# Seven block products instead of eight in the last ten slices of the first feed-forward

## The chip, the core and the metric

The kernel runs on one core of one Trainium2 chip. The metric is device time of one execution, in microseconds, as the median of three runs. TensorE (PE) multiplies; VectorE (DVE), ScalarE (ACT) and GpSimd (POOL) work on vectors; SyncE (SP) issues the DMAs.

## The reference

Windowed attention over 2 x 8 heads of 768 positions (windows of 96 keys and 24 block summaries), then two feed-forwards over the 1536 token rows of width 512 that it gives. The core of the reference, everything in float32:

```
h = x @ w_in          # 1536 x 512 by 512 x 2048
g = h * np.cos(h)     # first feed-forward
g = h * np.clip(h + 3.0, 0.0, 6.0) / 6.0   # second feed-forward
x = g @ w_out         # 1536 x 2048 by 2048 x 512
```

The weights come in as float64 in memory (512 KB for each slice of 128 x 512) and are brought to float32 on the chip by integer operations.

## The kernel before

**Precision and tiling.** Each float32 operand of a product is split into a high part in the engine's reduced float32 format and a rest ("hi" and "lo"), and a product is three passes: hi by hi, lo by hi, hi by lo. The 1536 token rows are three blocks of 512 (0, 1, 2); the inner width of 2048 is 16 slices of 128. A step is one slice by one block: its first product (12 matmuls of 512 columns into one PSUM bank, `mm1`), its middle (the nonlinearity, then the split of g, `middle`) and its second product (12 matmuls of 512 columns into four accumulators, `mm2`). Two steps make what the text calls a pair-block: two slices by one block.

**Groups and runs.** `GROUPS` cuts the 16 slices into groups; within a group all blocks are passed, forwards or backwards, and the four accumulators stay in PSUM for a run of steps of the same block. When a run closes, four "sums" add the accumulators to `total` in SBUF. The first group's steps on blocks 0 and 1 are made in halves of 256 columns while the attention still runs.

**Seven products.** The whole second feed-forward makes the first products of two slices together: the pair of weight slices and the block of x are each cut two by two, four sums of weights and four sums of x ("pair sums", "tees") are formed beforehand, and seven products of 256 columns (`mm1_set`, 7 x 6 matmuls) with one copy ("take") and five DVE additions ("add") give both slices' h in `hs`, in SBUF. The step `SETS` is the first one done so. Before it, h is read from PSUM directly.

**Order.** Nothing is written in its final order. Every operation is put into a graph with the engines that may run it and their costs; a planner gives each a due time from its successors plus a lead for its kind (`LEAD`, two numbers: before and after the attention's buffers are given up), and then forms every engine's queue by due time. Each engine runs its own queue strictly in order. Where the plan shows a gap on PE, filler matmuls of a zero tile are put in (`fill`); the threshold is a number in `run`. Of two engines that may run an operation (DVE or POOL, DVE or ACT) the planner chooses.

**Buffers.** Two pair buffers `phi`/`plo` hold the split weights of two pairs (or of six single slices), two buffers `raw`, `cv_y` and `cv_t` serve all weight conversions in turn, the g buffers number four plus one lent from `tx` (the sums of x), and in the sets h and c have four and three buffers.

The lines of the profile that the text names: L836 first products one slice at a time, L787 block products, L954 second products, L800 adds, L901 to L914 the middle of a step (turns, rest, cosine, gate, g hi, g lo), L487 to L515 the conversion of a weight slice, L455 its lo part, L472 pair sums, L741 to L754 tees, L924 and L929 fillers, L992 sums, L616 to L700 attention.

Of the kernel before, what the change touches and what calls it, by code (L numbers as in the profile page):

```python
# [36 lines left out]
class Graph:  # L37
# [18 lines left out]

    LEAD = {
        "add": (0.0, -9.5), "block product": (0.0, -0.9), "carry": (43.6, 0.3), "cosine": (2.4, 0.0),
        "flip": (1.4, 0.0), "g hi": (0.9, 0.0), "g lo": (0.4, -6.4), "gate": (2.3, 7.0), "gate six": (0.0, -60.9),
        "hi": (-2.2, -167.1), "identity": (4.0, 0.0), "inverse": (2.1, 0.0), "join": (5.5, 0.0),  # L60
        "key maxima": (165.5, 0.0), "largest": (-4.4, 0.0), "lo": (12.0, -0.3), "load v": (8.8, 0.0),
        "load window": (1.5, 0.0), "mask": (33.2, 0.0), "masks": (-4.3, 0.0), "means back": (5.9, 0.0),
        "means out": (-0.1, 0.0), "means over": (39.5, 0.0), "pair sums": (0.0, -72.4), "power": (5.3, 0.0),
        "put k": (-17.0, 0.0), "put v": (9.5, 0.0), "rebias": (-9.5, -7.7), "rest": (-30.7, 5.6),
        "scaled": (3.8, 0.0), "scores": (-2.4, 0.0), "second": (9.7, 15.7), "shift": (2.9, 0.0), "sign": (23.1, 4.6),
        "sums": (0.0, 1.4), "take": (0.0, 3.0), "tees": (0.0, -3.1), "tees hi": (0.0, 19.3), "tees lo": (0.0, 6.5),
        "turns": (0.0, 16.9), "wake": (4.4, 0.0), "weighted": (1.4, 0.0), "weights": (0.0, 0.6),
        "window": (253.9, 0.0), "x hi": (0.1, 0.0), "x lo": (-10.8, 0.0), "y lo": (0.0, -2.4),
# [87 lines left out]
    def replay(self, on, order):  # L156
# [8 lines left out]
        for _ in range(n):  # L165
            best = None
            for e, queue in queues.items():
# [7 lines left out]
                t = max(t, free.get(e, 0.0))  # L175
                if e == "POOL" or (e == "DVE" and self.twice[i]):
                    t = max(t, port)
                if best is None or t < best[0]:
                    best = (t, e, i)
            t, e, i = best  # L180
# [10 lines left out]
    def run(self):  # L191
# [17 lines left out]
        for i, j in zip(pe, pe[1:]):  # L209
            after[i] = max(0, int((begins[j] - ends[i] - 0.9) / mm(512)))  # L210
# [33 lines left out]
def attention_two_ffn(  # L244
# [32 lines left out]
    GROUPS = ((3, 3, 3, 3, 4), (4, 4, 4, 4))  # L277
    plan = []
    for m in range(2):
        f0 = 0  # L280
        for g, n in enumerate(GROUPS[m]):
            for b in range(NBLK) if (g + m * (len(GROUPS[0]) + 1)) % 2 == 0 else reversed(range(NBLK)):
# [9 lines left out]
    SETS = next(s for s in range(NSTEP) if plan[s][0])  # L292
# [164 lines left out]

    def convert_pair(p):

        if 2 * p >= len(slices):  # L460
            return
        i = p % NPAIR

        (y1, t1, y1k, t1k), (y0, t0, y0k, t0k) = nearest(2 * p, "in"), nearest(2 * p + 1, "in")
# [9 lines left out]
        for c0, c1, x, k in ((0, 2, y0.bitcast(F32), y0k), (2, 3, a22, y1k),  # L474
                             (3, 5, t0.bitcast(F32), t0k), (5, 7, t1.bitcast(F32), t1k)):
            hi, lo = (lambda t=t, c0=c0, c1=c1: t[i][:, c0:c1, :].rearrange("p a c -> p (a c)") for t in (phi, plo))
            also = [(n, "in", PER * i + f) for n in ("whi", "wlo") for f in range(PER)] if p < NF // 2 + NPAIR else []
# [123 lines left out]
    def front(u):  # L601
# [67 lines left out]
        G.op("inverse", {"DVE": 0.33}, inverse, r=[("sm", si)], w=[("rs", si)], twice=True)  # L669
# [97 lines left out]

    def mm1_set(s, due):

        m, blk, f, _, _ = plan[s]  # L770
        p = slices.index((m, f)) // 2
        i = p % NPAIR
# [299 lines left out]
    gone = set()  # L1072
# [20 lines left out]
    for what, s in events:  # L1093
# [16 lines left out]
        elif s == uses[m, f]:  # L1110
            now = s
            if n < NF - PER * NPAIR:
                convert(n + PER * NPAIR, "in")
            elif n < NF:

                gone.add(n % (PER * NPAIR))
                for i in range(NPAIR):
# [3 lines left out]
            elif n % 2:  # L1121
                convert_pair(n // 2 + NPAIR)
# [57 lines left out]
```

## Time and profile before

| | |
|---|---|
| median of 3 runs | 598.93 us (598.66 to 598.95) |
| the profiled execution | 598.99 us, span 597.2 us |
| mean granted clock of PE | 0.994 |
| PE busy | 582.4 us (98%) |
| DVE busy | 460.6 us (77%) |
| ACT busy | 344.1 us (58%) |
| POOL busy | 190.6 us (32%) |

Times within a trace are from the first instruction on. The first step in full width begins at about 94 us, the last attention unit's PE work ends at about 109 us, block products begin at 322 us, and the last matmul starts at 592.9 us. A busy time counts an instruction from its start to its end as recorded; since the next one on the same engine often starts before that end, the distance from start to start is the better price.

### The profile page before, as it was taken

The numbers are of one execution on the slowest core, as the hardware profiler recorded it, in microseconds if no ns is written. First come the engines' busy times: TensorE is split into PE (matmuls) and PEld (weight loads), VectorE is DVE, ScalarE is ACT, GpSimd is POOL, SyncE is SP. The second block draws the span as 40 slices with busy tenths as digits, with TensorE's granted clock in tenths as the row PEclk, the third lists the DMA queues.
The fourth block names the chain that finished last, engine by engine and source line by source line (L and its number), as shares of the span: only waits on it lengthen the run. The fifth ranks groups of instructions, "written<-read, shape, count | busy, mean of one in ns | idle before, by whom it ended". The sixth has DMA issues, their size and how long they took to land.

```text
span 597.2 us, 10065 instructions
## 1 busy us (share of the span) xinstructions
PE 582.4 (98%) x3818; PEld 498.8 (84%) x3818; DVE 460.6 (77%) x828; ACT 344.1 (58%) x721; POOL 190.6 (32%) x184
## 2 busy tenths in 40 slices
PE   9987999999999999999999999999999999999997
PEld 5666689888888888888888898989989889898985
DVE  5885898999877967755658998999998768963552
ACT  4887889787645635533447765667465445442320
POOL 4365544244403202101213554332534033411200
PEclk9988999999999999999999999999999999999999
DMA  8975323423412311301200220332322121100103
GB/s 308 308 250 167 99 89 91 154 69 137 134 37 70 107 36 35 106 1 36 71 1 1 72 65 7 106 106 72 141 68 75 70 72 36 37 0 1 54 37 124
DMA packets 17009, 51.51 MB, mean 86 GB/s; under 512 B 1984, under 2 KB 1984, under 8 KB 16960
## 3 DMA queue, kind: packets, MB, share of 16 engines
q1 hardware_dynamic: 16960, 50.86, 25.6%
q8 instruction: 30, 0.49, 0.3%
q14 instruction: 19, 0.16, 0.1%
HBM read 47.71 MB, written 3.15 MB: 85 GB/s over the span
## 4 chain that ended last, share of the span: by engine, by line
PE 89%; DMA 4%; DVE 3%; ACT 2%; issue 1%; SPq 0%; ACTq 0%; DVEq 0%
PE bank_a L954 22%; PE bank_d L836 12%; PE bank_d L787 10%; PE bank_b L954 10%; PE bank_c L954 10%; PE bank_c L787 5%; PE bank_e L787 5%; PE bank_c L836 5%; PE bank_e L836 5%; PE bank_e L700 2%; PE bank_b L685 2%; PE bank_c L629 1%; DMA raw<-in_w_out_dram 1%; DMA total<-in_vw_dram 1%; DMA raw<-in_w_in_dram 1%; DMA vnat<-in_vw_dram 1%
## 5 line engine op out<-in xcount | busy, mean ns | idle before, releaser
L515 POOL TENSOR_TENSOR cv_y<-cv_t,cv_y 128x512 int32<-128x512 int32 x30 | 43.3, 1449 | 90.8 <-DVE cv_t L513 61.9
L914 POOL TENSOR_TENSOR glo<-ch_c,ghi 128x512 fp32r<-128x512 f32 x21 | 28.3, 1348 | 123.8 <-PE bank_c L954 69.3
L438 ACT CAST ghi<-ch_c 128x512 fp32r<-128x512 f32 x57 | 35.4, 620 | 47.9 <-PE bank_c L954 47.1
L513 DVE SCALAR_TENSOR_TENSOR cv_t<-raw,cv_t 128x512 int32<-128x512 int32 x64 | 48.6, 769 | 0.4
L908 ACT ACTIVATE ch_c<-hs,three 128x512 f32<-128x512 f32 x48 | 34.5, 722 | 18.9 <-DVE hs L800 18.5
L506 ACT ACTIVATE cv_t<-raw 128x512 f32<-128x512 f32 x52 | 35.0, 676 | 16.4 <-DMA raw<-in_w_out_dram 7.4
L496 ACT ACTIVATE cv_y<-raw 128x512 int32<-128x512 uint32 x53 | 35.4, 673 | 14.5 <-POOL wlj_out L455 5.2
L910 DVE SCALAR_TENSOR_TENSOR ch_c<-ch_c,hs 128x512 f32<-128x512 f32 x48 | 40.3, 846 | 2.7 <-ACT ch_c L908 2.4
L800 DVE TENSOR_TENSOR hs<-bank_d,hs 128x256 f32<-128x256 f32 x60 | 25.1, 419 | 20.7 <-PE bank_d L787 19.9
L914 DVE TENSOR_TENSOR glo<-ch_c,ghi 128x512 fp32r<-128x512 f32 x44 | 35.4, 806 | 1.4 <-PE bank_c L954 0.9
L836 PE MATMUL bank_d<-xlo,phi 128*128 128x512 f32 (+1 forms) x136 | 35.6, 358 | 0.0
L836 PE MATMUL bank_d<-xhi,phi 128*128 128x512 f32 (+1 forms) x136 | 32.3, 360 | 2.4 <-DVE ch_e L905 2.2
L511 DVE TENSOR_SCALAR cv_t<-cv_t 128x512 int32<-128x512 int32 x64 | 29.5, 468 | 2.7 <-ACT cv_t L506 2.7
L836 PE MATMUL bank_d<-xhi,plo 128*128 128x512 f32 (+1 forms) x136 | 31.5, 356 | 0.0
L836 PEld LDWEIGHTS bank_d<-xhi,phi 128*128 128x128 f32 x136 | 23.4, 193 | 6.4 <-DVE ch_e L905 2.5
L660 ACT ACTIVATE es<-bank_c,nmx 128x120 f32<-128x120 f32 x80 | 27.6, 370 | 1.8 <-DVE nmx L653 1.6
L515 DVE CUSTOM_DVE_ANT_0 cv_y<-cv_t,cv_y 128x1024 uint16<-128x1024 uint16 x34 | 26.2, 772 | 2.2 <-ACT cv_y L496 2.1
L836 PEld LDWEIGHTS bank_d<-xlo,phi 128*128 128x128 f32 x136 | 23.8, 193 | 3.7 <-issue 0.2
L992 DVE SCALAR_TENSOR_TENSOR total<-bank_a,total 128x512 f32<-128x512 f32 x22 | 14.8, 686 | 15.5 <-PE bank_a L954 15.3
L836 PEld LDWEIGHTS bank_d<-xhi,plo 128*128 128x128 f32 x136 | 23.4, 193 | 3.5
L455 POOL TENSOR_TENSOR plo<-cv_y,phi 128x512 fp32r<-128x512 f32 (+1 forms) x16 | 19.8, 1238 | 15.1 <-ACT phi L438 14.4
L903 ACT ACTIVATE ch_c<-ch_c,half_pi 128x512 f32<-128x512 f32 x25 | 18.1, 722 | 9.1 <-DVE ch_c L901 9.1
(348 smaller groups left out, 1838.2 us busy)
## 6 DMA issues: line engine op xcount, KB each, us to landing
raw<-in_w_in_dram SPq DMA_DIRECT2D x32, 512.0 KB, 3.3
raw<-in_w_out_dram SPq DMA_DIRECT2D x32, 512.0 KB, 3.3
vcat<-in_vw_dram SPq DMA_DIRECT2D x12, 384.0 KB, 4.6
ktile<-in_kt_dram SPq DMA_DIRECT2D x8, 384.0 KB, 5.9
qt<-in_q_dram SPq DMA_DIRECT2D x12, 256.0 KB, 4.3
out_dram<-total SPq DMA_DIRECT2D x8, 256.0 KB, 2.0
total<-in_vw_dram SPq DMA_DIRECT2D x6, 256.0 KB, 6.2
out_dram<-totak SPq DMA_DIRECT2D x4, 256.0 KB, 2.0
```

Of the source, the lines that this page charges most:

```text
L438: nc.scalar.copy(o, i) if e == "ACT" else VEC[e].tensor_copy(o, i)
L496: nc.scalar.activation(y, low.bitcast(U32), AF.Copy, scale=2.0 ** -29)
L506: nc.scalar.activation(o, a, AF.Copy, scale=2.0 ** -112)
L511: G.op("shift", {"DVE": dve(DM, 2)}, lambda e: nc.vector.tensor_scalar(t, t, 3, None, ALU.logical_shift_left), w=[tk], twice=True)
L513: G.op("sign", {"DVE": dve(DM)}, lambda e: nc.vector.scalar_tensor_tensor(t, high, -0x80000000, t, ALU.bitwise_and, ALU.bitwise_or), r=[rk ...
L515: G.op("join", {"POOL": pool(DM), "DVE": dve(DM)}, lambda e: VEC[e].tensor_tensor(y, t, y, ALU.add), r=[tk], w=[yk], twice=True)
L787: nc.tensor.matmul(o, wt[i][:, A[a], kk * P:(kk + 1) * P], xt[:, kk, :], start=first and n + kk == 0, stop=n + kk == 3, skip_group_check=True)
L836: nc.tensor.matmul(h, w["in"][i][:, kk * P:(kk + 1) * P], x[blk][:, kk, c0:c1], start=p + kk == 0, stop=p == 2 and kk == NK - 1)
L908: G.op("relu", {"ACT": act(N) + 0.1}, lambda e: nc.scalar.activation(c(), h(), AF.Relu, bias=three), r=hk, w=ck)
L910: G.op("gate six", {"DVE": dve(N)}, lambda e: nc.vector.scalar_tensor_tensor(c(), c(), 6.0, h(), ALU.min, ALU.mult), r=hk, w=ck, twice=boo ...
L914: G.op("g lo", {"DVE": dve(N), "POOL": pool(N)}, lambda e: VEC[e].tensor_tensor(gbuf("lo", s)[:, 0:N], c(), gh().bitcast(F32), ALU.subtrac ...
L954: nc.tensor.matmul(acc(s, i)[0], l, r, start=first, stop=end and p == 2 and (N == TOK or i % 2 == 1), skip_group_check=N < TOK)
```

## The change

Ten of the 16 slices of the first feed-forward are made by pairs as in the second: `WHOLE` = 6 slices stay single, and `SETS` moves from the first step of the second feed-forward to the first step of slice 6. The groups become 3, 3, 4, 2, 4; the blocks' direction is a table (`BACKWARD`), so that the second and third group start at block 0 again. The sums of x for the first feed-forward are formed from the hi and lo parts of x (`tees_of_parts`), in the buffers that the second feed-forward uses later. The lent g buffer is used up to four steps ahead of `SETS`. `inverse` is two operations instead of one. The planner lets an operation take the port that DVE and POOL share 0.055 us early, breaks ties by when an operation was ready, has other leads for its kinds, and puts fillers into gaps from 0.3 us beyond a filler's own length instead of 0.9.

```
+    HANDED = 0.055
     LEAD = {
-        "add": (0.0, -9.5), "block product": (0.0, -0.9), "carry": (43.6, 0.3), "cosine": (2.4, 0.0),
+        "add": (0.0, -116.7), "block product": (0.0, 0.3), "carry": (6.7, 17.2), "cosine": (-4.2, -220.4),
...
                 if e == "POOL" or (e == "DVE" and self.twice[i]):
-                    t = max(t, port)
+                    t = max(t, port - self.HANDED)
...
-            after[i] = max(0, int((begins[j] - ends[i] - 0.9) / mm(512)))
+            after[i] = max(0, int((begins[j] - ends[i] - 0.3) / mm(512)))
...
-    GROUPS = ((3, 3, 3, 3, 4), (4, 4, 4, 4))
+    GROUPS = ((3, 3, 4, 2, 4), (4, 4, 4, 4))
+    BACKWARD = ((0, 0, 0, 1, 1), (1, 0, 1, 0))
+    WHOLE = GROUPS[0][0] + GROUPS[0][1]
...
-    SETS = next(s for s in range(NSTEP) if plan[s][0])
+    SETS = next(s for s in range(NSTEP) if plan[s][0] or plan[s][2] >= WHOLE)
...
-        def inverse(e):
-            nc.vector.tensor_scalar(sme, sm, 1.0e-9, None, ALU.add)
-            nc.vector.reciprocal(rs, sme)
+        G.op("sum", {"DVE": 0.13}, lambda e: nc.vector.tensor_scalar(sme, sm, 1.0e-9, None, ALU.add),
+             r=[("sm", si)], w=[("sme", si)], twice=True)
...
+    def tees_of_parts(b, ts):
...
+        if 2 in ts:
+            chain(2, [(part(xhi, 1, 1), part(xhi, 0, 1), sub), (temp(2), part(xlo, 1, 1), add),
+                      (temp(2), part(xlo, 0, 1), sub)])
+        if 1 in ts:
+            chain(1, [(temp(2), part(xhi, 0, 0), add), (temp(1), part(xlo, 0, 0), add)])
+        for t, k in ((2, None), (1, None), (3, (1, 0)), (0, (1, 1))):
...
+                chain(t, [(part(xhi, *k), temp(1), sub), (temp(t), part(xlo, *k), add)])
+            parts(t)
...
-                gslot[s] = next(k for k in free if k < (NGL if s < SETS else NG1))
+                gslot[s] = next(k for k in free if k < (NGL if s < SETS - LAG1 - 1 else NG1))
...
+            if n < WHOLE:
+                if n % PER == PER - 1:
+                    convert_pair(n // PER)
+            elif (n - WHOLE) % 2:
+                convert_pair(pair(n) + NPAIR)
...
+        if what == "used" and m == 0 and f == WHOLE - 1:
+            tees_of_parts(b, (3, 0) if b == LENT[0] else (2, 1, 3, 0))
+            if plan[s + 1][1] == LENT[0]:
+                tees_of_parts(LENT[0], (2, 1))
```

PE's queue where a slice beyond the sixth meets a block of x. First before: one step's first product on block 2, between the second products of earlier steps (xhi and xlo are the parts of x, ghi and glo those of g).

```order
L954 MATMUL bank_b<-glo_1531,whi_out_73 128x512
L954 MATMUL bank_c_96<-glo_1531,whi_out_73 128x512
L836 MATMUL bank_c_97<-xhi_87,phi_69 128x512 x4
L836 MATMUL bank_c_97<-xhi_87,plo_71 128x512 x4
L836 MATMUL bank_c_97<-xlo_90,phi_69 128x512 x2
L954 MATMUL bank_a_93<-ghi_1528,whi_out_74 128x512
L954 MATMUL bank_a_94<-ghi_1528,whi_out_74 128x512
L836 MATMUL bank_c_97<-xlo_90,phi_69 128x512 x2
```

And of the change, the same place on block 0, the first pair (L836 is now the block product, txhi and txlo the sums of x, L1003 the second product).

```order
L836 MATMUL bank_d_99<-txhi_1569,phi_69 128x256 x2
L836 MATMUL bank_d_99<-txhi_1569,plo_71 128x256 x2
L836 MATMUL bank_d_99<-txlo_1572,phi_69 128x256 x2
L1003 MATMUL bank_a_93<-ghi_1561,whj_out_1553 128x512
L1003 MATMUL bank_a_94<-ghi_1561,whj_out_1553 128x512
L1003 MATMUL bank_a_93<-ghi_1561,wlj_out_1555 128x512
L1003 MATMUL bank_a_94<-ghi_1561,wlj_out_1555 128x512
L1003 MATMUL bank_a_93<-glo_1565,whj_out_1553 128x512
L1003 MATMUL bank_a_94<-glo_1565,whj_out_1553 128x512
L836 MATMUL bank_d_99<-xhi_85,phi_69 128x256 x2
L836 MATMUL bank_d_99<-xhi_85,plo_71 128x256 x2
L836 MATMUL bank_d_99<-xlo_88,phi_69 128x256 x2
```

Twelve matmuls of 512 columns for each slice became six of 256 for each of seven products, and the products of one bank follow each other after a few second products. In all, 360 matmuls of 512 columns leave PE's queue and 630 of 256 enter it.

DVE's queue where the first such set is added up, in the change (L849 are the adds, hs the buffers of h, L950 is rest, L954 gate, L522 the join and L520 the sign of a weight conversion, L788 a tee, L458 a lo part).

```order
L849 TENSOR_TENSOR hs_1576<-bank_d_99,hs_1575 128x256
L522 ISA cv_y_81<-cv_t_83,cv_y_81 128x1024
L788 TENSOR_TENSOR hs_1578<-xhi_87,hs_1577 128x512
L849 TENSOR_TENSOR hs_1575<-bank_d_99,hs_1575 128x256
L849 TENSOR_TENSOR hs_1575<-bank_e,hs_1575 128x256
L458 TENSOR_TENSOR plo_72<-cv_y_81,phi_70 128x512
L849 TENSOR_TENSOR hs_1575<-bank_d_99,hs_1575 128x256
L849 TENSOR_TENSOR hs_1576<-bank_e,hs_1576 128x256
L950 SCALAR_TENSOR_TENSOR ch_c_1557<-hs_1575,ch_c_1557 128x512
L950 SCALAR_TENSOR_TENSOR ch_c_1558<-hs_1576,ch_c_1558 128x512
L520 SCALAR_TENSOR_TENSOR cv_t_84<-raw_68,cv_t_84 128x512
```

The adds are new in this place, they stand between conversions and tees, and rest reads h from SBUF instead of from a bank.

The same stretch of PE's queue in the attention, after the first x is there, before and then of the change (L685 and L690 transposes, L616 and L623 masks, L700 and L705 weighted values, zero the fillers).

```order
L836 MATMUL bank_d_98<-xlo_88,phi_69 128x256 x4
L836 MATMUL bank_d_99<-xhi_85,phi_69 128x256 x4
L836 MATMUL bank_d_99<-xhi_85,plo_71 128x256 x4
L836 MATMUL bank_d_99<-xlo_88,phi_69 128x256 x4
L685 MATMUL bank_b<-ident,es_134 120x128 x8
L616 MATMUL bank_c_96<-mask_hi,ident_r 128x480
```

```order
L973 MATMUL bank_d_99<-zero 128x512 x4
L690 MATMUL bank_b<-ident,es_134 120x128 x4
L885 MATMUL bank_d_99<-xhi_85,phi_69 128x256 x4
L690 MATMUL bank_b<-ident,es_134 120x128 x4
L885 MATMUL bank_d_99<-xhi_85,plo_71 128x256 x4
L885 MATMUL bank_d_99<-xlo_88,phi_69 128x256 x4
```

Fillers of 512 columns went from 10 to 28 and of 256 from 2 to 6. All but two of them stand before the last attention unit; those two stand in the merged run of block 2 in the first feed-forward's third and fourth group.

## Rows read from the trace of the kernel before

**Rows 1.** Page: busy time, share of the span; then PE and its clock in 40 slices.
```profile
PE 582.4 (98%) x3818; PEld 498.8 (84%) x3818; DVE 460.6 (77%) x828; ACT 344.1 (58%) x721; POOL 190.6 (32%) x184
...
PE   9987999999999999999999999999999999999997
...
PEclk9988999999999999999999999999999999999999
```

**Rows 2.** Chain of waits in order of time: start us, us, what.
```profile
43.99 6.98 DMA raw<-in_w_out_dram
...
54.07 2.64 PE bank_d L836 x12
...
115.53 2.72 PE bank_e L836 x12
...
120.97 5.44 PE bank_d L836 x24
...
322.25 0.71 PE bank_e L787 x6
322.96 0.72 PE bank_c L787 x6
...
592.69 1.37 DVE total L992 x2
```

**Rows 3.** What PE waited for, longest first: us in total, times, longest.
```profile
PE bank_d L836 <- DVE ch_e L905: 2.2, 1, 2.2
PE bank_b L685 <- POOL es L670: 1.7, 1, 1.7
...
PE bank_e L787 <- ACT hs L438: 0.9, 1, 0.9
...
PE bank_d L787 <- DVE plo L455: 0.2, 1, 0.2
```

**Rows 4.** Timeline of PE: first matmul of three block-product sets (start us, us).
```profile
471.44 0.28 PE L787 MATMUL bank_d<-xhi,phi 128*128 128x256 f32 x1
...
481.98 0.28 PE L787 MATMUL bank_c<-xhi,phi 128*128 128x256 f32 x1
...
492.52 0.28 PE L787 MATMUL bank_e<-xhi,phi 128*128 128x256 f32 x1
```

**Rows 5.** Windows: PE, PEld, DVE, ACT, POOL busy us (instructions), PE clock, DMA share, GB/s.
```profile
50.00:60.00 10.00, 6.58 (x63) 6.14 (x63) 5.96 (x14) 7.85 (x23) 7.00 (x7) 0.83 0.30 89
340.00:360.00 20.00, 20.00 (x131) 18.13 (x131) 18.07 (x33) 12.68 (x24) 12.57 (x10) 1.00 0.17 54
400.00:420.00 20.00, 20.00 (x137) 18.48 (x136) 18.96 (x35) 14.38 (x27) 7.82 (x7) 1.00 0.30 100
440.00:460.00 20.00, 20.00 (x126) 17.99 (x125) 18.41 (x34) 10.38 (x21) 9.30 (x8) 1.00 0.28 98
```

**Rows 6.** Timeline of DVE, second feed-forward: start us, us, instruction.
```profile
421.00 0.41 DVE L800 TENSOR_TENSOR hs<-bank_d,hs 128x256 f32<-128x256 f32 x1
421.33 0.41 DVE L800 TENSOR_TENSOR hs<-bank_e,hs 128x256 f32<-128x256 f32 x1
421.66 0.67 DVE L515 CUSTOM_DVE_ANT_0 cv_y<-cv_t,cv_y 128x1024 uint16<-128x1024 uint16 x1
422.28 0.69 DVE L910 SCALAR_TENSOR_TENSOR ch_c<-ch_c,hs 128x512 f32<-128x512 f32 x1
422.89 0.42 DVE L508 TENSOR_SCALAR cv_t<-raw 128x512 f32<-128x512 f32 x1
```

**Rows 7.** Timeline of POOL and DVE: waiting for the shared port, and a short POOL operation.
```profile
127.73 1.29 POOL L515 TENSOR_TENSOR cv_y<-cv_t,cv_y 128x512 int32<-128x512 int32 x1 [2.36 <-ACT txhi L438]
128.11 1.47 DVE L914 TENSOR_TENSOR txlo<-ch_c,txhi 128x512 fp32r<-128x512 f32 x1
...
129.50 0.68 DVE L905 TENSOR_TENSOR ch_c<-bank_d,ch_c 128x512 f32<-128x512 f32 x1
...
294.58 0.75 POOL L472 TENSOR_TENSOR cv_t<-cv_y,cv_t 128x256 f32<-128x256 f32 x1 [2.69 <-DVE cv_t L472]
```

More of the change, by code (lines that the diff above doesn't have):

```diff
@@ L55 @@
     UNWANTED, SWITCH = 1.0, 8.0
+    HANDED = 0.055
     LEAD = {
-        "add": (0.0, -9.5), "block product": (0.0, -0.9), "carry": (43.6, 0.3), "cosine": (2.4, 0.0),
[L59 to L68, printed above, removed]
+        "add": (0.0, -116.7), "block product": (0.0, 0.3), "carry": (6.7, 17.2), "cosine": (-4.2, -220.4),
+        "first": (-53.2, -2.5), "flip": (-1.5, 0.0), "g hi": (2.7, 7.6), "g lo": (-6.7, 0.0), "gate": (-0.5, -0.8),
+        "gate six": (0.0, 1.0), "half sums": (-0.4, 0.0), "hi": (-143.8, -2.4), "identity": (-9.1, 0.0),
+        "inverse": (-7.8, 0.0), "join": (0.0, -0.7), "lo": (-19.9, 0.7), "load k": (-8.7, 0.0), "mask": (-9.8, 0.0),
+        "means": (2.6, 0.0), "means back": (4.3, 0.0), "means out": (2.1, 0.0), "means over": (-4.9, 0.0),
+        "negative": (-2.5, 0.0), "power": (-1.9, 0.0), "put k": (30.7, 0.0), "rebias": (0.0, 8.2),
+        "relu": (0.0, -31.9), "rest": (0.0, -1.8), "scaled": (-1.0, 0.0), "shift": (-11.0, 0.0), "sign": (1.0, 9.0),
+        "store": (0.0, -4.8), "sum": (-309.7, 0.0), "switch": (0.0, -6.1), "take": (0.0, -128.3),
+        "tees hi": (0.0, -6.8), "turns": (8.0, -1.4), "wake": (7.1, 0.0), "weighted": (6.0, 0.0),
+        "weights": (-1.1, -17.2), "window": (-6.2, 0.0), "x lo": (1.4, 0.0), "y hi": (0.0, 5.2),
     }
@@ L765, in tees, with part, temp, chain @@
         parts(0, b22, down)
+    def tees_of_parts(b, ts):
+        n = 2 * HALF
+        spare = {t: NH - 2 if t == 1 else NH - 1 for t in range(4)}
+        def part(x, k, t):
+            return (lambda: quarter_of(x[b], k, t).bitcast(F32)), xkeys("xh" if x is xhi else "xl", b, k, t)
+        def temp(t):
+            i = spare[t]
+            return (lambda: hs[i].rearrange("p (a c) -> p a c", a=2)), [("h", i, 0), ("h", i, 1)]
+        def chain(t, steps):
+            o, ok = temp(t)
+            for (x, xk), (y, yk), op in steps:
+                G.op("tees", {"POOL": pool(n), "DVE": dve(n)}, lambda e, x=x, y=y, op=op: VEC[e].tensor_tensor(
+                    o(), x(), y(), op), r=[*xk, *yk, "room"], w=ok, twice=True)
+        def parts(t):
+            x, r = temp(t)
+            if t < 3:
+                hi, lo = (lambda: tx["hi"][b][:, t]), (lambda: tx["lo"][b][:, t])
+                hk, lk = [("th", b, t)], [("tl", b, t)]
+                if (b, t) == LENT:
+                    hk, lk = hk + [("gh", NG1)], lk + [("gl", NG1)]
+            else:
+                hi, lo = (lambda: quarter_of(xhi[b], 0, 1)), (lambda: quarter_of(xlo[b], 0, 1))
+                hk, lk = xkeys("xh", b, 0, 1), xkeys("xl", b, 0, 1)
+            G.op("tees hi", {"ACT": act(n), "DVE": dve(n, 2), "POOL": one(n)}, lambda e: copy(e, hi(), x()), r=r, w=hk, twice=True)
+            G.op("tees lo", {"POOL": pool(n), "DVE": dve(n)}, lambda e: VEC[e].tensor_tensor(
+                lo(), x(), hi().bitcast(F32), ALU.subtract), r=[*r, *hk], w=lk, twice=True)
+        add, sub = ALU.add, ALU.subtract
+        if 2 in ts:
[4 more added lines that the diff above has]
+        for t, k in ((2, None), (1, None), (3, (1, 0)), (0, (1, 1))):
+            if t not in ts:
+                continue
+            if k:
+                chain(t, [(part(xhi, *k), temp(1), sub), (temp(t), part(xlo, *k), add)])
+            parts(t)
     def mm1_set(s, due):
         m, blk, f, _, _ = plan[s]
-        p = slices.index((m, f)) // 2
-        i = p % NPAIR
+        i = pair(slices.index((m, f))) % NPAIR
         (x, xk), (y, yk), (w, wk) = (hbank(s, k) for k in range(3))
```

32 lines of the change are left out of this document (12 added, 20 removed).

## The prediction

> **What bounds the kernel now.** I read the page first: PE is busy for 98% of the span, at full clock in nearly every slice, and no other engine comes near it over the whole span [rows 1]. A busy PE need not be a PE at its best, so next comes the pace. On the chain of waits twelve first products of 512 columns take 2.72 us and 24 take 5.44 us, 0.227 us each, and six block products of 256 columns take 0.71 to 0.72 us, 0.119 us each [rows 2]. From about 60 us on these paces hold without a break: the list of what PE waited for [rows 3] adds up to 10.9 us in eleven waits, and only two of them, 0.9 and 0.2 us, lie behind the attention. So from there on the time is PE's own work in line, and one microsecond taken from it is one microsecond of the span, as long as the other engines keep up. Before 60 us PE does wait. The longest wait, 2.2 us, is for a gate of DVE, and right behind it twelve products of 256 columns take 2.64 us instead of 1.43, with a mean granted clock of 0.83 in that window, so part of it ran at 1.2 GHz [rows 2, 3, 5]. Behind the last matmul stand two sums and their stores, some 4 us [rows 2]; they are the same in both kernels.
>
> **The sum, step by step,** against the profiled execution: 598.99 us, span 597.2, so 1.8 us outside; it lies 0.06 us above the median of 598.93.
>
> *First products of ten slices.* A pair-block made directly costs 2 x 12 x 0.227 = 5.44 us of PE, by seven products 42 x 0.119 = 5.02; 0.42 less. Measured with the second products around it, three sets of the second feed-forward start 10.54 us apart [rows 4], where the direct form takes 5.44 + 5.44 = 10.88: 0.34 less, because a matmul of 512 right behind one of 256 starts a little late. Five pairs by three blocks are 15 pair-blocks: 5.1 us by the one, 6.3 by the other. In the new order the products of a set stand in longer runs, which means fewer such changes; but I stay near the pace that is measured in place: **-5.4 us**. TensorE: Matmul & The Clock Gate (the Trainium skill, "Back-to-back issue gap") gives a lone matmul N/2.4 ns plus 2.5 ns; by that a pair-block would save 0.59 us and fifteen 8.9. The trace gives both sizes here, and both are slower than the rule, so its sum is not used.
>
> *Vector work that this buys.* Each of the 15 sets adds five adds and two takes; each block nine tees and four splits into hi and lo; each pair four pair sums and a larger split; and the second and third group no longer continue the block before them, which makes three more run closings, 12 sums. Between the first add and the first gate of the second feed-forward I count DVE's queue in the new order: with operands in SBUF alone 129 operations of 512 and 34 small ones (256 columns, or 512 at the double rate); with a PSUM operand 82 small ones and 32 of 512. Successive starts on DVE lie 0.33 us apart behind a 256 and 0.61 behind a 512, and 0.33 is near what I take for the small ones in general [rows 6]. In SBUF alone: 129 x 0.61 + 34 x 0.33 = 90 us; with PSUM 82 x 0.33 + 32 x 0.61 = 47. Together 137 us. PE's time for the stretch is 15 x 10.5 plus some 6 us until the first gate of the second feed-forward: 163. DVE alone fits, at 84%. POOL has 48 operations of 512, 20 of 256 and two casts there: 48 x 1.29 + 22 x 0.75 = 78 us [rows 7].
>
> *The shared port.* While POOL runs its join, a DVE operation on SBUF that started beside it is recorded with 1.47 us instead of 0.68 and ends 0.56 us after POOL's end; the next one, with a PSUM operand, is back to 0.68 [rows 7]. So POOL's work and DVE's work on SBUF stand in one line: 90 + 78 = 168 us in 163. But the waiting operation ends 0.05 us sooner behind POOL than its pitch of 0.61 says, and POOL's 1.29 overlaps in the same way; with some sixty changes of hands I reckon the line at about 162. That is full. SBUF — State Buffer (the Trainium skill, "SBUF: two separate sides") says that the pair of ports is an exclusive lock, that whoever starts first keeps it for the whole instruction and that the loser fully blocks. By that rule the sum would be the 168, 5 us more than PE has; the row agrees on the lock, but shows the hand-over earlier than the end as recorded.
> What has the trace to say on such density? Recorded DVE and POOL time together were 54.5 us in the two windows from 400 and from 440 us, 1.36 for each us, and 30.6 us in the window from 340, 1.53, and PE ran through all three [rows 5]. The new stretch, priced as recorded (0.68 and 0.42 for DVE, as above for POOL), has 158 + 78 = 236 us in 163: 1.45. So it asks for longer what the trace shows for 20 us at a time. Behind the window from 340 PE waited 0.9 us [rows 3]. Bounds: nothing, or such a 0.9 in each of eight stretches of 20 us, 7 us. I take two of them: **+1.7 us**, since the one window of that density ran free and was followed by one wait. What is queued behind a late add is the whole of DVE's line, and PE waits at the next product of the same bank.
>
> *Takes and the ACT queue.* Two more ACT copies of 256 in each set, priced like the add at 0.41: 0.8 us of 10.5, on an engine that is busy 10.4 to 14.4 of 20 us in the dense windows [rows 5]. Hidden; without cover 12 us in all, but ACT would have to be full first.
>
> *Weights and buffers.* The first two pairs' buffers fall free at the ends of the first and second group; the first pair is wanted a whole group later, the second one pair-block later, as every pair in the second feed-forward is. One buffer of g less from four steps ahead of SETS: four remain for a lag of three steps. Both at nothing, covered by 10 us of PE work each; if that cover goes, a split of 1.3 us is late once.
>
> *Fillers.* 18 more of 512 columns and four of 256 make 18 x 0.227 + 4 x 0.119 = 4.6 us of PE work, all but 0.45 us of it before the last attention unit, in gaps that the planner sees. They cost nothing where PE waits anyway. If none of the gaps were there they cost 4.6. That only one gap in the whole paired stretch got fillers means the planner sees none other over 0.53 us there; that is its order and no time, and I give it little weight.
>
> *The start.* All leads are new, and so is the order of the DMAs on SP's queue (the means of v come ahead of the first weights), of the conversions on ACT, DVE and POOL, and of PE's early work: the first product now stands ahead of the fifth unit's scores. What can be won is the 2.2 us wait and the 1.2 us lost to the low clock right behind it, 3.4 us; what can be lost is another pair like it, since a weight load of 6.98 us stands on the chain there [rows 2, 3]. I take **-0.5**, nearest to nothing, on the winning side because more fillers leave PE less long without work ahead of the products.
>
> Sum: -5.4 + 1.7 - 0.5 = -4.2 us, 598.99 - 4.2 = 594.8 for an execution like the profiled one, **594.7 us** against the median.
>
> **The rivals.**
> *The port decides (slower).* If 1.36 is what can be kept up, as in the two longer dense windows, the paired stretch needs 236/1.36 = 174 us, 11 over its 163, from its third block on: 598.93 - 5.9 + 11 = 604 us. For it: both engines' counts, and the lock that the rows show; the Trainium skill's rule above is of this kind. Against it: the window of 1.53.
> *Late adds (no change).* The products of one bank now follow each other closer, in all 39 sets. If each loses 0.15 us of PE behind an add, half of one small operation's pitch, that is 5.9 us and all of the gain: 598.9 us. For it: adds stand behind tees and conversions in one queue. Against it: the second feed-forward waited only 1.1 us in 24 sets.
> *The start gains in full.* -5.4 - 3.4 and no new waits: 590.1 us. For it: fillers between the transposes, where the clock had dropped. Against it: PE waits there for other engines, and more pace on PE does not bring those forward.
> *The start loses.* +3.4 instead of -0.5: 598.6 us. For it: the DMA order puts the first weight slice behind the means; against it: the bytes up to there are the same.
>
> **How the numbers follow.** Forecast 0.48 (own range 592.5 to 597), port 0.14, late adds 0.13, start gains 0.14, start loses 0.10; 0.01 is left for more than one at once. A change of 0.2%, 1.2 us, is about what a measurement of this kernel can tell from none, so faster is under 597.7 and slower over 600.1. Faster: forecast 0.47, start gains 0.14, and a third of late adds and of start loses, 0.08, and 0.02 of a mild port: 0.71. Same: 0.14 from the two cases that end at 598.6 and 598.9 and the forecast's edge. Slower: port 0.12, the rest from the upper halves of those two: 0.15. The range goes from the start's gain, 590.3, to 600.5; beyond it are the port and little else.
>
> **What would show it.** Right: sets 10.4 to 10.6 us apart in the paired stretch, the first product of the second feed-forward's first set some 4 to 5 us sooner relative to the last attention unit, PE's waits behind 110 us under 4 us in all, DVE over 90% and POOL near 45% busy as recorded in that stretch. Wrong: sets 11 us or more apart with waits of PE for adds or lo parts (port), many waits of 0.1 to 0.3 us at block products in both feed-forwards (late adds), or a last attention unit that ends more than 2 us away from 109 us (the start). The whole is wrong if the paired stretch is not PE's own pace.

## The result and the profile after

The changed kernel takes 590.77 us (median of 4 runs, 589.87 to 591.34), the kernel before 598.79 us beside it (598.20 to 598.95): a ratio of 0.9866, 95% interval 0.9849 to 0.9884. The forecast was 594.7. The measured time lies 0.5 us inside the lower end of the range, 590.3. The profiled execution took 590.25 us, span 588.5, which is 8.7 less than the span before. Among the executions further down one stands apart, 1994 us of "fillers back"; it is the one that was traced, so that kernel is read by its five other times only.

The page of the changed kernel, the same three rows as [rows 1]:
```profile
PE 579.1 (98%) x4110; PEld 508.3 (86%) x4110; DVE 497.7 (85%) x913; ACT 379.2 (64%) x798; POOL 246.1 (42%) x230
...
PE   9989999899999999999999999999999999999997
...
PEclk9999999999999999999999999999999999999999
```
DVE is busy for 37 us more, POOL for 56, and PE is the bound as before. The clock row has no 8 left. What PE waited for:
```profile
PE bank_e L705 <- ACT pts L441: 1.2, 2, 0.8
PE bank_b L690 <- ACT pts L441: 1.2, 2, 0.7
PE bank_d L530 <- DVE zero L379: 1.1, 1, 1.1
PE bank_d L885 <- ACT xhi L441: 0.7, 1, 0.7
PE bank_c L636 <- DMA qt<-in_q_dram: 0.5, 1, 0.5
PE bank_e L836 <- DVE hs L441: 0.2, 1, 0.2
```
The 2.2 us for a gate and the 0.9 us in the second feed-forward [rows 3] are gone. Two waits lie behind the attention: 0.7 us for xhi, right at its end, and 0.2 us. Windows of the changed kernel (columns as in [rows 5]): two of the start, the stretch between the attention and the first pairs, the paired stretch, the second feed-forward.
```profile
30.00:40.00 10.00, 8.65 (x130) 6.94 (x128) 8.92 (x17) 8.26 (x27) 5.41 (x6) 1.00 0.88 303
50.00:60.00 10.00, 10.00 (x149) 9.11 (x149) 9.21 (x21) 9.97 (x30) 4.21 (x5) 1.00 0.47 142
...
110.00:170.00 60.00, 60.00 (x277) 50.14 (x276) 54.55 (x84) 39.57 (x66) 38.46 (x29) 1.00 0.13 46
170.00:330.00 160.00, 159.68 (x1001) 144.11 (x1001) 149.99 (x269) 109.73 (x196) 75.54 (x62) 1.00 0.19 66
330.00:570.00 240.00, 240.00 (x1504) 217.15 (x1503) 191.63 (x348) 132.66 (x240) 82.54 (x66) 1.00 0.18 63
```
The same in the kernel before:
```profile
30.00:40.00 10.00, 7.45 (x90) 5.79 (x89) 8.32 (x20) 8.16 (x26) 6.54 (x6) 0.83 0.77 261
...
170.00:330.00 160.00, 160.00 (x727) 133.32 (x726) 113.23 (x181) 81.14 (x131) 32.21 (x25) 1.00 0.14 46
330.00:570.00 240.00, 238.92 (x1493) 214.88 (x1492) 194.03 (x356) 128.92 (x237) 82.10 (x63) 1.00 0.18 61
```
In the paired stretch DVE and POOL together went from 145 to 226 us in 160, from 0.91 to 1.41 for each us, while PE lost almost nothing. Between 110 and 170 us they recorded more, 93 us in 60 or 1.55 for each us, and PE was busy throughout. Four set starts of the paired stretch (timeline of PE):
```profile
221.16 0.40 PE L836 MATMUL bank_c<-xhi,phi 128*128 128x256 f32 x2
...
231.69 0.40 PE L836 MATMUL bank_e<-xhi,phi 128*128 128x256 f32 x2
...
242.19 0.40 PE L836 MATMUL bank_d<-xhi,phi 128*128 128x256 f32 x2
...
252.71 0.40 PE L836 MATMUL bank_d<-xhi,phi 128*128 128x256 f32 x2
```
10.52 us apart, the pace of [rows 4]. And the end of the attention, its last product with v, before and then after:
```profile
107.64 1.15 PE L700 MATMUL bank_e<-pts,vcat 120*64 120x64 f32 x32
```
```profile
105.51 1.15 PE L705 MATMUL bank_e<-pts,vcat 120*64 120x64 f32 x30 [0.42 <-ACT pts L441]
```
Behind it comes the first product of a step in full width, before (109.90 us, not the 94 us given under the time before) and after:
```profile
109.90 1.09 PE L836 MATMUL bank_d<-xhi,phi 128*128 128x512 f32 x4
```
```profile
107.33 1.20 PE L885 MATMUL bank_d<-xhi,phi 128*128 128x512 f32 x4 [0.68 <-ACT xhi L441]
```

**Where the 8.7 us came from.** I cut both timelines at the start of that row's last matmul (108.57 and 106.43 us), at the first block product of the second feed-forward, and at the last matmul. A stall is the elapsed time less the count of matmuls by 0.2267 us for 512 columns and 0.12 for 256; so it holds waits and small losses between matmuls alike.

| part | forecast | measured | from |
|---|---|---|---|
| first products of ten slices | -5.4 | -6.0 | 360 fewer of 512, 630 more of 256 |
| stalls in the first feed-forward | +1.7 | +2.3 | 0.24 to 2.56 |
| fillers there | 0 | +0.45 | 2 more of 512 |
| stalls in the second feed-forward | not counted | -2.3 | 3.23 to 0.95 |
| start, up to the last attention product | -0.5 | -3.2 | -2.1, with 9 products of 256 (1.1 us) more ahead of it |
| sum | -4.2 | -8.7 | |

Of the 2.56 us of stalls in the first feed-forward 0.9 lie right at the cut, at the wait for xhi, and 1.5 between 170 and 330 us, where the kernel before lost nothing.

### The profile page after: what moved, and what is told of

It reads as the page before. It is cut to its first block, busy times and chain, and to the rows that moved or that the text cites. A ratio compares the mean times of both kernels' runs of the same rounds, so it can differ in the third digit from the quotient of the medians.

```text
span 588.5 us, 10756 instructions
## 1 busy us (share of the span) xinstructions
PE 579.1 (98%) x4110; PEld 508.3 (86%) x4110; DVE 497.7 (85%) x913; ACT 379.2 (64%) x798; POOL 246.1 (42%) x230
## 4 chain that ended last, share of the span: by engine, by line
PE 92%; ACT 4%; DMA 2%; DVE 1%; issue 0%; ACTq 0%
PE bank_a L1003 24%; PE bank_d L836 17%; PE bank_b L1003 10%; PE bank_c L1003 10%; PE bank_c L836 8%; PE bank_e L836 8%; PE bank_d L885 5%; PE bank_e L705 1%; PE bank_c L885 1%; PE bank_e L885 1%; PE bank_e L581 1%; ACT es L667 1%; PE bank_c L636 1%; PE bank_b L690 1%; DMA raw<-in_w_out_dram 1%; PE bank_d L530 1%
## 5 line engine op out<-in xcount | busy, mean ns | idle before, releaser
L522 POOL TENSOR_TENSOR cv_y<-cv_t,cv_y 128x512 int32<-128x512 int32 x38 | 52.4, 1380 | 88.0 <-DVE cv_t L520 60.1
L849 DVE TENSOR_TENSOR hs<-bank_d,hs 128x256 f32<-128x256 f32 x100 | 42.1, 422 | 23.0 <-PE bank_d L836 21.6
L441 ACT CAST ghi<-ch_c 128x512 fp32r<-128x512 f32 x82 | 50.0, 618 | 14.4 <-DVE ch_c L959 8.4
L520 DVE SCALAR_TENSOR_TENSOR cv_t<-raw,cv_t 128x512 int32<-128x512 int32 x64 | 51.2, 809 | 0.1
L458 POOL TENSOR_TENSOR plo<-cv_y,phi 128x512 fp32r<-128x512 f32 (+1 forms) x19 | 22.1, 1163 | 43.4 <-DVE phi L441 26.2
L441 ACT COPY hs<-bank_d 128x256 f32<-128x256 f32 x37 | 13.8, 373 | 30.7 <-PE bank_d L836 30.2
L849 DVE TENSOR_TENSOR hs<-bank_c,hs 128x256 f32<-128x256 f32 x48 | 20.3, 423 | 13.4 <-PE bank_c L836 12.6
L836 PE MATMUL bank_d<-xlo,phi 128*128 128x256 f32 x156 | 31.4, 283 | 0.0
L836 PE MATMUL bank_d<-xhi,phi 128*128 128x256 f32 x156 | 31.4, 283 | 0.0
L836 PE MATMUL bank_d<-xhi,plo 128*128 128x256 f32 x156 | 31.4, 282 | 0.0
L849 DVE TENSOR_TENSOR hs<-bank_e,hs 128x256 f32<-128x256 f32 x47 | 19.9, 422 | 12.2 <-PE bank_e L836 11.5
L836 PEld LDWEIGHTS bank_d<-xhi,phi 128*128 128x128 f32 x156 | 26.4, 190 | 3.7 <-DVE hs L849 1.0
L948 ACT ACTIVATE ch_c<-hs,quarter 128x512 int32<-128x512 f32 x30 | 21.3, 723 | 12.1 <-DVE hs L849 11.5
```

What stands on the lines that cost most here:

```text
L441: nc.scalar.copy(o, i) if e == "ACT" else VEC[e].tensor_copy(o, i)
L520: G.op("sign", {"DVE": dve(DM)}, lambda e: nc.vector.scalar_tensor_tensor(t, high, -0x80000000, t, ALU.bitwise_and, ALU.bitwise_or), r=[rk ...
L522: G.op("join", {"POOL": pool(DM), "DVE": dve(DM)}, lambda e: VEC[e].tensor_tensor(y, t, y, ALU.add), r=[tk], w=[yk], twice=True)
L836: nc.tensor.matmul(o, wt[i][:, A[a], kk * P:(kk + 1) * P], xt[:, kk, :], start=first and n + kk == 0, stop=n + kk == 3, skip_group_check=True)
L849: G.op("add", {"DVE": dve(HALF)}, lambda e: nc.vector.tensor_tensor(o[0](), a, b[0](), ALU.add), r=[ak, b[1], "room"], w=[o[1]])
```

## The experiments

Each ratio is against runs of the kernel before on the same chip. First, on the start. My theory was that the new early leads (the number in force up to the hand-over) had won it.

**Early leads back.** In the changed kernel:
```
-        "carry": (6.7, 17.2), "cosine": (-4.2, -220.4), "first": (-53.2, -2.5), ...
+        "carry": (43.6, 17.2), "cosine": (2.4, -220.4), "first": (0.0, -2.5), ...
```


> The changed kernel, with the early number of every lead (the one in force up to the hand-over from attention to feed-forward) put back to the kernel before; pairs, late leads, filler bound and buffers stay changed. Theory: the start won some 3.3 us and the early leads won it; then this takes 590.8 + 3.3 = 594, and its first full-width first product starts near 109.9 us and not 107.3. Rival 1: the start won through the fillers, which keep the clock up; then this stays at 590.8 with the first product near 107.3. Rival 2: the start won nothing of its own and the whole gain is in the pairs; 590.8 as well, but with the first product near 109.9 and PE's lost time less behind it.

604.4 us, ratio 1.009 (1.006 to 1.013): not 3.3 but 13.6 us over the changed kernel. The last attention product starts at 117.48 us instead of 106.43; behind it the kernel takes 479.7 us against 477.8. The new late leads keep their worth; the start is lost.

**Early leads alone.** In the kernel before:
```
-        "carry": (43.6, 0.3), "cosine": (2.4, 0.0), "gate": (2.3, 7.0), ...
+        "carry": (6.7, 0.3), "cosine": (-4.2, 0.0), "first": (-53.2, 0.0), "gate": (-0.5, 7.0), ...
```


> The kernel before, with only the early number of every lead from the changed kernel. Theory (early leads won 3.3 us): 598.8 - 3.3 = 595.5, first full-width first product near 107 us. Rival (fillers, or the new form only): 598.8 and 109.9 us. If early leads and fillers each need the other, also 598.8.

609.8 us, ratio 1.018 (1.015 to 1.022), the last attention product at 116.06 us: 11 us slower, where I expected 3.3 faster. My theory falls as stated. The crossing is not quite clean: the kernel before makes in one operation, `inverse`, what the changed kernel makes in two, and it was given the lead of the other part, `sum` (-309.7), not that of `inverse` (-7.8). The next kernel has the same; what this does to the time was not tried.

**All planning numbers alone.** The kernel before, its products unchanged, with all leads, the allowance, the tie-break and the filler bound of the changed one:
```
+    HANDED = 0.055
-        "add": (0.0, -9.5), "block product": (0.0, -0.9), "carry": (43.6, 0.3), ...
+        "add": (0.0, -116.7), "block product": (0.0, 0.3), "carry": (6.7, 17.2), ...
-            after[i] = max(0, int((begins[j] - ends[i] - 0.9) / mm(512)))
+            after[i] = max(0, int((begins[j] - ends[i] - 0.3) / mm(512)))
```


> The kernel before, without the new pairs, with all of the changed kernel's planning numbers (leads of both kinds, allowance at the port, filler bound 0.3). Theory: the start's 3.3 us come without the pairs, and the second feed-forward loses about 1 us less, so 598.8 - 3.3 - 1 = 594.5. Rival 1: the numbers fit the new program alone: 598 or more. Rival 2: they win only the second feed-forward's waits: 597.5.

608.6 us, ratio 1.018 (1.014 to 1.022), the last attention product at 117.11 us: rival 1. But its second feed-forward stalls for 1.74 us where the kernel before has 3.23, so some 1.5 of the 2.3 us won there come with the planning numbers alone. What PE waited for up to 125 us, and one window at the end of the attention:
```profile
PE bank_b L689 <- POOL es L674: 3.4, 1, 3.4
...
PE bank_b L689 <- DVE es L674: 1.1, 1, 1.1
```
```profile
110.00:120.00 10.00, 6.50 (x45) 5.01 (x46) 4.27 (x6) 2.41 (x5) 1.79 (x1) 0.55 0.01 2
```
At the end of the attention PE waits for the softmax of the last units, its clock falls (0.55), and the other engines are idle for more than half of the window too; I read it as units that came too late as a chain. The three crossed kernels (the last three), and the pairs with old numbers below, start the last attention product at 116 to 119 us, and the kernels whose early leads belong to their program at 105 to 109 (110.6 with the double dose of POOL work below). ACT's table loads agree: each crossed kernel has one more pair of them.
```profile
L957 ACT ACT_TABLE_LOAD x8 | 10.3, 1283 | 0.1
L672 ACT ACT_TABLE_LOAD x7 | 9.0, 1283 | 1.1 <-DVE nmx L665 1.0
```
These are of "early leads back", up to 125 us; the changed kernel:
```profile
L952 ACT ACT_TABLE_LOAD x7 | 9.0, 1283 | 0.1
L667 ACT ACT_TABLE_LOAD x6 | 7.7, 1283 | 0.2 <-DVE nmx L660 0.2
```
That is 2.6 of some 10 us of ACT's time; whether PE feels it was not tested. Which of the many leads does the rest wasn't separated.

**Fillers back**, in the changed kernel, and **fillers alone**, in the kernel before; one number in each:
```
-            after[i] = max(0, int((begins[j] - ends[i] - 0.3) / mm(512)))
+            after[i] = max(0, int((begins[j] - ends[i] - 0.9) / mm(512)))
```


> The changed kernel with the filler bound put back from 0.3 to 0.9 us: fewer products that only keep TensorE busy. Theory (leads, not fillers, won the start): 590.8, within 0.5 us, the clock at its upper level in the windows from 30 and from 50 us. Rival (fillers keep the clock up): the granted clock falls to about 0.83 in one of the two windows and the time is 592 to 594.

> The kernel before with the filler bound of 0.3 us instead of 0.9 and nothing else. Theory (fillers are near neutral): 598.8, within 0.5 us. Rival (fillers keep the clock up): 596 to 597.6, the granted clock in the windows from 30 and 50 us at 1.00 instead of 0.83. If fillers cost what they take of PE: up to 603.

Fillers back: ratio 0.988 (0.984 to 0.991), its five times 589.6 to 594.2 with a median of 591.5. Fillers alone: 599.4 us, ratio 1.001 (0.998 to 1.005). So the bound moves nothing that can be measured in time; whether the clock held in the two windows, as my expectation for "fillers back" asked, could not be read for want of a usable trace (the mean clock was 0.997 to 1.0). The profiled execution of "fillers alone" is of use in another way: it kept its clock,
```profile
30.00:40.00 10.00, 9.49 (x113) 7.52 (x112) 8.29 (x21) 9.88 (x35) 5.99 (x6) 1.00 0.95 315
50.00:60.00 10.00, 8.09 (x108) 6.95 (x106) 7.68 (x17) 9.46 (x26) 6.88 (x8) 1.00 0.34 117
```
took 596.1 us and had its last attention product at 105.68, 2.9 us sooner than the kernel before in its profile. Its first product in full width comes sooner than even that of the changed kernel (107.33):
```profile
107.00 1.09 PE L836 MATMUL bank_d<-xhi,phi 128*128 128x512 f32 x4
```
Others of the same kernel, at a mean clock of 0.994, took 599.4 to 602.0. The clock, then, is what comes and goes in the start of this program, and where it holds, the old order's start is as short as the new one's.

**The changed kernel again, and without fillers.** The second sets the filler to nothing; 34 filler products went, and the 12 ahead of the first real work stayed, which the expectation had counted in.
```
-            if after.get(i) and self.filler:
+            if after.get(i) and self.filler and False:
```


> The changed kernel unchanged, beside the kernel before on the same chip. Theory (the start's gain is the clock, which the changed kernel never loses): granted clock 1.00 in nearly every run and 590 to 591.5, while the kernel before spreads from 594 at clock 1.00 to 601 at 0.994. Rival (the chips of the other runs are simply less even): the changed kernel spreads over 6 us too.

> The changed kernel without any filler product (46 of them left out, 9.8 us of PE work; they compute nothing). Theory (fillers keep the clock through the start): the granted clock falls in the windows between 20 and 60 us, the last product of the attention ends 3 us or more after 106.4, 594 to 600. Rival (PE only fills time that it would wait anyway and the clock does not depend on them): 590.8, clock 1.00.

The changed kernel again: 591.5 us (590.3 to 592.7), clock 0.999 or 1.0 in all five runs; the kernel before ran on that chip at 593.4 to 601.7 with the clock from 0.997 to 0.989. The theory holds as to the evenness: the changed kernel is even, the kernel before isn't. (The kernel before had its 593.4 at a clock of 0.997, though, not 1.00.) Without fillers: 592.4 us, ratio 0.990 (0.986 to 0.994), the last attention product at 106.67, clock 1.00 in every window of the start of its profile. So the fillers are worth about 1 us at most (591.7 to 594.5 us against 590.3 to 592.7), most of it behind the attention, and do not keep the clock: the rival, which had asked for 590.8.

**The pairs with all old planning numbers.** Now the paired stretch. Edit: the changed kernel with both numbers of every lead, no allowance, and the filler bound as before.
```
-    HANDED = 0.055
+    HANDED = 0.0
-        "add": (0.0, -116.7), "block product": (0.0, 0.3), "carry": (6.7, 17.2), ...
+        "add": (0.0, -9.5), "block product": (0.0, -0.9), "carry": (43.6, 0.3), ...
```


> The changed kernel's pairs, buffers and group order, with all of the kernel before's planning numbers: both numbers of every lead, no allowance at the port, filler bound 0.9 us. Theory (products alone are worth 5.4 us, and the late leads remove the port's waits): 598.8 - 5.4 = 593.4, plus 1 to 5 us of waits in the paired stretch which the late leads had been set to remove, so 594 to 598. Rival 1 (the port is not near its limit, whatever the order): 593 to 594. Rival 2 (the port decides without the new order): over 599.

622.0 us, ratio 1.042 (1.038 to 1.046): rival 2 and beyond. The start ends at 118.6, and PE stalls for 8.0 us in the first and 10.4 in the second feed-forward, with 21 fillers (4.8 us) beside. The tie-break stayed changed; like the allowance it moves only where fillers stand.

**Late leads back**, and nothing else, which tells these two losses apart:
```
-        "add": (0.0, -116.7), "cosine": (-4.2, -220.4), "take": (0.0, -128.3), ...
+        "add": (0.0, -9.5), "cosine": (-4.2, 0.0), "take": (0.0, 3.0), ...
```


> The changed kernel with the late number of every lead (the one in force in the feed-forwards) put back to the kernel before; early leads, allowance at the port, filler bound, pairs stay changed. Theory (the port is full and the late leads' order is what keeps PE free of it): PE loses some 12 us between 170 and 470 us as in the pairs with all old numbers, so 600 to 604, the last product of the attention still near 106.4. Rival (the allowance at the port or the fillers did that): under 593.

607.7 us, ratio 1.016 (1.011 to 1.021), with the last attention product at 106.36, as in the changed kernel. That is beyond the 600 to 604 of the theory, and far from the rival. Behind the attention PE stalls for 3.1 us in the first and 8.8 in the second feed-forward and runs 22 and 11 fillers (7.5 us) where the planner itself saw gaps; together 15.4 us over the changed kernel there. Only 5.1 of them fall in the first feed-forward: between 170 and 330 us PE stalls for 2.0 us, against 1.5 in the changed kernel. 10.3 fall in the second, most of them in its first sets. (Its first block product starts at 331.5 us.) That is the worst place; here by the waits of PE from 330 to 360 us, one window, and the chain there (start us, us, what):
```profile
PE bank_d L883 <- ACT phi L488: 2.0, 1, 2.0
PE bank_d L883 <- DVE plo L505: 1.4, 2, 0.8
```
```profile
330.00:350.00 20.00, 16.84 (x96) 14.10 (x95) 18.58 (x35) 11.67 (x22) 6.42 (x4) 1.00 0.16 52
```
```profile
340.98 0.69 DVE ch_c L1006
341.67 1.71 DVE glo L1010
343.39 1.71 DVE cv_y L569
345.09 0.60 DVE glo L1010
345.69 0.60 DVE cv_t L567
```
And POOL's timeline beside it:
```profile
341.54 1.30 POOL L806 TENSOR_TENSOR txlo<-total,txhi 128x512 fp32r<-128x512 f32 x1 [2.37 <-ACT txhi L488]
342.80 1.75 POOL L811 TENSOR_TENSOR total<-total 128x512 f32<-128x512 f32 x1
```
The chain runs down DVE's queue, one operation behind the other. Two of them took 1.71 us on it instead of 0.60: each ends some 0.5 us after the POOL operation beside it, like the held one in [rows 7]. The lo part of a weight pair stands at the end of that line, and PE waits for it. DVE isn't out of work; since nothing but the late leads differs, it is the order that brings the lo part late.

**No allowance at the port.**
```
-    HANDED = 0.055
+    HANDED = 0.0
```


> The changed kernel with the allowance of 0.055 us at the port put back to nothing: the planner's replay then sets begin times a little later, which moves only where fillers stand. Theory (late leads carry the paired stretch): 590.8, within 0.6 us. Rival (the allowance carries it): 594 or more, with waits of PE between 170 and 370 us.

590.6 us, ratio 0.986 (0.982 to 0.991): the same. The allowance carries nothing that can be measured. What the late leads carry is mostly the way into the second feed-forward, and less of the paired stretch than I had thought.

**How full the port is.** The changed kernel with POOL work added in each of the 15 sets, two small additions in one kernel and four in the other:
```
+            for d in range(2 if m == 0 else 0):
+                G.op("extra", {"POOL": pool(HALF)}, lambda e: nc.gpsimd.tensor_tensor(
+                    extra, extra, extra, ALU.add), w=["extra"], due=when(s) + 3.0 + 2.0 * d, at=when(s), twice=True)
```


> The changed kernel with work added: two additions of 256 columns on a small tile of zeros on POOL in each of the fifteen sets of the paired stretch, some 30 x 0.75 = 22 us of POOL and of the shared port. Theory that counts the port as full (162 of 163 us): 22 us have no room, so the time rises by 15 to 22 us, to 606 to 613. Theory that the waits term was priced too high because the order spreads the work and DVE's pitch behind POOL is shorter than counted: room for some 10 to 20 us is left, and the time rises by 0 to 6, to 591 to 597.

> The same with four such additions in each set, some 45 us of POOL. Port full from the start: 590.8 + 38 to 45 = 629 to 636. Room for 10 to 20 us: 616 to 626. If POOL's work did not hold the port against DVE at all and only POOL's own time counted (48 operations of 512, 20 of 256 and these 60 make about 123 of 163 us): below 595.

608.9 and 624.6 us, 18 and 34 over the changed kernel. Of the first, its POOL group, the waits of PE from 279 to 291 us, and the window:
```profile
L1157 POOL TENSOR_TENSOR extra<-extra 128x256 f32<-128x256 f32 x30 | 23.9, 797 | 0.9
```
```profile
PE bank_e L838 <- ACT phi L443: 3.1, 1, 3.1
PE bank_d L838 <- ACT hs L443: 1.8, 1, 1.8
```
```profile
170.00:330.00 160.00, 148.84 (x900) 132.70 (x899) 143.51 (x246) 100.19 (x177) 86.50 (x73) 0.97 0.19 63
...
284.00:294.00 10.00, 6.92 (x27) 6.20 (x28) 8.66 (x19) 5.42 (x10) 5.45 (x4) 0.51 0.25 82
```
23.9 us of POOL cost 18 us of time, within the 15 to 22 of the theory that counted the port as full. Not all of the 18 is waiting for the line. Around the longer of the two waits PE was busy for 6.92 of 10 us at about half its clock, which by an estimate from that row lost 3.4 us, and five more fillers took 1.1. The first wait is put down to an ACT copy, but the chain there runs through DVE without a gap:
```profile
284.08 0.68 DVE total L1043
284.76 0.60 DVE cv_y L524
285.36 0.34 DVE plo L460
285.69 1.00 DVE cv_t L481 x3
286.70 0.61 DVE plo L460
...
287.35 1.24 PE bank_e L838 x4
```
The double dose, 46 us of POOL, costs 34. Its 624.6 us lie inside the range of the other theory (room for 10 to 20 us: 616 to 626) and 4 us under that of "full from the start". So the two doses speak for different theories, and neither for one in which POOL's work costs PE nothing (below 595). The double dose runs 33 fillers more than the changed kernel (7.5 us of the 34), gaps that the planner saw. And there is a rival that I did not test: an added operation changes the planner's order too, under leads that were set without it, and such a mismatch cost 11 to 15 us above with no work added.

Recorded DVE and POOL time for each us of the window is 1.44 with the two additions and 1.39 with the four, 1.42 in "late leads back" and in the pairs with old numbers, 1.41 in the changed kernel. That is no ceiling: the changed kernel holds 1.55 from 110 to 170 us without a wait of PE, as shown with the windows of the result.

No kernel here beats the changed one beyond what can be measured.

## Why the prediction was right, and where it was not

The time of 590.77 us is just inside the range (590.3 to 600.5), and under the 592.5 to 597 that I gave to the forecast itself: the change was worth 8.0 us where I had 4.2. The largest part, the first products, I had nearly right; what doubled the gain is the start and the second feed-forward.

*What bounds the kernel.* Right: behind the attention the time is PE's own work in line, and the 6.0 us of products taken from it came off the span but for the stalls in the table.

*First products.* Right in mechanism and near in size: -6.0 for -5.4, between the 5.1 and 6.3 that I had as bounds. I took the pace with the changes between 512 and 256 columns in it; in longer runs those losses were fewer, as the text had said and not priced. My reason for them was inexact: from 335 to 570 us a 512 behind a 256 starts on time (0.120 us) in both traces, and it is the distance from it to the next 512 that is longer: 0.233 to 0.234 us, where 0.227 to 0.229 is usual.

*The shared port.* Right in size: I counted 162 of 163 us, asked for a recorded density of 1.45, and took +1.7; the stretch ran at 1.41, with DVE busy for 94% and POOL for 47% of it, and PE's stalls there rose from nothing to 1.5 us. Whether the line was as full as I counted stays open: the added POOL work shows little room, but not none, and it does not tell the port from a disturbed order. The rule of the Trainium skill that I set beside it (SBUF — State Buffer, "SBUF: two separate sides", on the shared port pair as an exclusive lock), applied to every DVE operation on SBUF alone, would have put 168 us of work in 163; the changed kernel kept within some 2 us of PE's pace, so as a sum it asked too much, while as a lock it agrees with the 1.71 us rows above. The rival "port decides" has a wrong ceiling: 1.36, where the changed kernel held 1.41 for 160 us and 1.55 for 60. What I had not seen is how much is a matter of the order: with the old late leads the same program loses 15 us, though 10 of them behind the paired stretch.

*Second feed-forward.* Missed: 2.3 us less stall there. I read its waits as 1.1 us, which is what the list names; counted against the pace the loss was 3.2. The two waits are gone, and part of the rest is that products of 256 columns follow products of 512 there 107 times before and 50 times after. The diff changes the late leads there too, and I priced them only for the paired stretch.

*Late adds.* No sign of them: sets 10.52 us apart, and stalls of the second feed-forward under 1 us in 24 sets.

*Takes, weights, buffers, fillers.* Nothing, as priced; the fillers behind the attention cost 0.45 us.

*The start.* This is the step that failed: "I take -0.5, nearest to nothing". It won 3.2 of the 3.4 us that I had as its bound; both windows in which the clock had been at 0.83 ran at 1.00, and the gate's wait went. My own marker said so: the last attention unit ends at 106.7, more than 2 us from 109. The reason that I gave for half a us, fillers, is wrong; without fillers the start is as short. The 3.2 us go almost wholly with the clock: the old order with its clock kept, in the trace of "fillers alone", starts its first product in full width at 107.00 us, the new one at 107.33. So the new start is not a shorter one; it is one that kept its clock, at a mean of 0.998 to 1.0, in all 14 executions of the changed kernel and of the one without the allowance. Why it does is not shown. Leads set for another program lose the start by 10 us and more, but the split of `inverse`, the order of the DMAs and each single lead were not tried by themselves. The time came out where the rival "start gains in full" had it (590.1), in part by luck: that rival's "no new waits" is false, and 2.3 us of new stalls in one feed-forward happen to stand against 2.3 won in the other.

*The marker at the second feed-forward.* I had written 4 to 5 us sooner relative to the last attention unit. Its first product stands 220.1 us behind it, against 213.5 before; but 48 more second products (10.9 us) and 9 fewer of half size (1.1) lie in between, so it comes 3.2 us sooner.

How much of that is the new order and how much is chance stays open. Runs of the kernel before with a mean clock of 0.999 or 1.0 took 593.8 to 595.3 us, against 589.6 to 591.5 for "fillers back" at such a clock on the same chip, and 590.3 to 592.7 for the changed kernel on another: against the kernel before at its best the change is worth some 3 to 4 us, against its common time 8. That is less than the 5.5 us that the feed-forwards won in the table, so at its best the old start may even be the shorter one; no trace shows it. Why the old program keeps its clock in some executions only was not tried.

## What to carry to other kernels

Where a planner sets the order, price its numbers with the program as one: the same early leads end the attention's products at 106 us in their own program and at 116 in the other, and the same products are worth -8 us with their own numbers and +23 with the old ones. Before a prediction, count stalls against the pace (elapsed less count by pitch) in every stretch that the new numbers reach, not only in the one where the edit is: the list of waits showed a third of them. And read how many fillers the planner placed: the order of "late leads back" has 33 of them behind the attention, the changed kernel's has two, so the planner's own replay would have told the two apart before any run. And before a gain in a start is put down to an edit, compare executions of equal clock.

## What the runs showed of the hardware

The kernel before has no fixed time: 593.4 to 603.0 us over 45 executions on three chips. It goes with the mean granted clock, but not by it alone (0.999 and 1.0: 593.8 to 595.3; 0.996 and 0.997: 593.4 to 598.8; 0.994: 598.1 to 601.6). In its trace the drop is in two windows of the start at 0.83, by estimate 1.7 us of PE's work each and 3.4 at most; the trace without the drop has its attention 2.9 us sooner. In these traces long waits went with matmuls at the lower level: 2.2 us and 0.83 [rows 3, 5], 3.4 us and 0.55, 3.1 us and 0.51 above.

DVE and POOL together recorded 1.39 to 1.44 us of work for each us over 160 us in the four kernels whose order or added work made PE wait (1.39 with the double dose, 145.59 and 77.32 us). It is not what they can hold at most: in the changed kernel 1.55 for 60 us, with PE busy throughout. A recorded time holds the waiting for the other engine too, like the 1.71 us instead of 0.60 above, so such a density is no measure of a full line.
